# Layer-norm rows of an MLP's token blocks turned by VectorE and DMAs instead of TensorE, in an fp32 adaLN block on one core

## The chip, the cores and the metric

The kernel runs on one core of a Trainium2 chip. The metric is the device time of one execution in microseconds (us). Three runs of the kernel before gave a median of 1103.63 us (1103.35 to 1103.67).

## What is computed

One transformer block with adaptive layer norms, on 2048 tokens of width 448, in fp32. The part that matters here is its second half:

```python
h = _layernorm(x, axis=-1) * (1 + cb) + sb          # x: 2048 x 448
y = _layernorm(h, axis=-1)                          # a second norm, inside the MLP
g = _gelu(jnp.einsum("bsd,df->bsf", y, w1) + b1)    # F = 1792
x = x + gb * (jnp.einsum("bsf,fd->bsd", g, w2) + b2)
```

The first half is a softmax attention with 16 heads of 28 columns over all 2048 tokens. Its code and its order are not touched by the change.

## The kernel before, in words

**Tiling.** The 2048 tokens are four blocks of 512 (`b` = 0 to 3), and a block is four tiles of 128 tokens (`t`). The residual rows of a block stay in SBUF in `acc[b]`, tokens on partitions. Every fp32 product is made of two fp32r parts, a rounded `hi` and a rest `lo`, as three products: hi·hi, hi·lo and lo·hi.

**The MLP phase** runs from about 792 us to the end. The list `seq` has 56 steps, 14 per block: step `n` is block `b`, slice `i` of the hidden width. In a step TensorE first does `mlp1(b, i)`, 11 matrix products (L396) of the turned rows `yT[b]` with a slice of w1, and then `mlp2`, 12 products (L1438 to L1440), for the slice of two steps earlier (`LAG = 2`). Between them, off TensorE: ScalarE applies the GELU to the PSUM tile of `mlp1` (L1394), then `hi` is copied (L1397, on ScalarE in block 0, on VectorE in blocks 1 to 3) and VectorE subtracts to get `lo` (L1398). At a block's last slice, which falls in step 1 of the next block, VectorE adds the four PSUM tiles of `mlp2` to `acc[b]` (L1444) into buffers `xn`, and SyncE stores them (L1445). The PSUM pair tiles `s1` and `s0` are then free for `mlp2` of the next block, which starts in step 2.

**The rows of the next block** are prepared by `ln2_stages(b + 1)`, whose `stage(i)` is called in step `i` of block `b`. In the table `plan`: `stat(0, t)` takes the statistics of `acc` (L200, L201), with the reciprocal root on GpSimd (L207) after the fourth; `mid(t)` normalises (L217) and GpSimd multiplies by `1 + cb` and adds `sb` (L1123, L1124); `stat(1, t)` and `fin(t)` do the second norm, and `fin` copies the last 64 columns once more to columns 448 to 511 (L1129); `addb(t)` lets GpSimd add the row `b2·gb` to `acc` (L1132). An instruction goes to its engine's queue in the order of the program and starts when its own waits are over.

**Turning the rows.** `mlp1` needs features on partitions. `chunk(k)`, for `k` = 0 to 3, takes 128 columns: four TensorE transposes with an identity into one PSUM tile (L277), then ScalarE's copy to `hi` (L1155) and VectorE's subtract to `lo` (L1157, L1159; for `k` = 3, where only 64 columns are real, `hi` fills the lower 64 partitions and `lo` the upper 64). In a block's step 13, chunks 0 and 1 stand on TensorE between `mlp1` and `mlp2`, and chunks 2 and 3 after `mlp2`, ahead of the next block's first `mlp1`.

**Weights.** In block 0 the last slices of w1 and w2 are still being prepared, one or two items a step, by `w_prep.step()`: SyncE loads rows into one of three buffers `raw` (L1175 to L1178 for w1, L1196 for w2). For w1 ScalarE copies `hi` (L1187) and VectorE subtracts (L1188). For w2 VectorE multiplies by `gb` (L1206), ScalarE copies `hi` (L1208) and VectorE subtracts (L1209). The last two of the 30 items are rows of w2, in steps 12 and 13.

**Buffers.** Four buffers `xn` go round for the normalised rows and for the output rows. The buffer `slot_e1` holds half of the attention's output weights until the last `project` in step 8 of block 0.

Of the kernel before, what the change touches and what calls it, by code (L numbers as in the profile page):

```python
# [13 lines left out]
F32 = mybir.dt.float32  # L14
F32R = mybir.dt.float32r
AF = mybir.ActivationFunctionType
ALU = mybir.AluOpType
# [5 lines left out]
D = 448  # L23
# [3 lines left out]
NC = 4  # L27
NB = S // 512
# [16 lines left out]
def tile_adaln_block(ctx: ExitStack, tc: tile.TileContext, x, wqkv, wo, w1, b1, w2, b2, c, w_mod, out):  # L45
    nc = tc.nc
    pe, act, dve, pool, sp = nc.tensor, nc.scalar, nc.vector, nc.gpsimd, nc.sync
# [13 lines left out]
    def ps_tile(key, n=1):  # L61
        return ps_pools[key][1].tile([128, 512], F32, tag=key, name=nm(key), bufs=n)
# [7 lines left out]
    dr = ctx.enter_context(tc.tile_pool(name="dr", bufs=1, space=DRAM))  # L70
# [47 lines left out]
    def f(t):  # L118
        return t.bitcast(F32)
# [78 lines left out]
    def ln_stat(mv, t, src):  # L198
        st = sbt("st", [128, 6], bufs=2)
        dve.bn_stats(out=st, in_=src)  # L200
        dve.bn_aggr(out=mv[:, t, :], in_=st)  # L201

    def ln_rstd(mv, n):
        ve = sbt("ve", [128, 4], bufs=2)
        dve.tensor_scalar(out=ve[:, :n], in0=mv[:, :n, 1], scalar1=EPS, scalar2=None, op0=ALU.add)
        rs = sbt("rs", [128, 4], bufs=2)
        pool.tensor_tensor(out=rs[:, :n], in0=ve[:, :n], in1=neg_half[:, :n], op=ALU.pow)  # L207
        return [(mv[:, t, 0:1], rs[:, t : t + 1], rs) for t in range(n)]
# [7 lines left out]
    def normalise(dst, src, mr):  # L216
        dve.tensor_scalar(out=dst[:, :D], in0=src, scalar1=mr[0], scalar2=mr[1], op0=ALU.subtract, op1=ALU.mult)  # L217

    def xn_t():
        return sbt("xn", [128, 512], bufs=4)  # L220
# [54 lines left out]
    def transposes(p, xs, k):  # L275
        for t in range(4):
            pe.transpose(p[:, t * 128 : (t + 1) * 128], xs[t][:, k * 128 : (k + 1) * 128], ident)  # L277
# [40 lines left out]
    for k in range(NC):  # L318
        for j in range(2):
            rs_, cs = mod_part(k, j, 2)  # L320
# [413 lines left out]


    rows = {}
    drow = dr.tile([4, D], F32, tag="drow", name="drow", bufs=1)

    mod = {}
# [65 lines left out]
    for n, i in (  # L805
# [7 lines left out]
        p, ts = firsts[n]  # L813
# [3 lines left out]
    for b in range(NB):  # L817
# [12 lines left out]
        for n, (tb, kind, g) in enumerate(tasks):  # L830
# [9 lines left out]
            k = n - (6, 4, 4, 4)[b]  # L840
# [5 lines left out]
            if kind < 2:  # L846
                fn = qk_task(tb, kind, g, firsts[n] if b == 0 and n < 3 else None)
# [254 lines left out]
    yT = {}  # L1102

    def ln2_stages(b):
        h2 = []
        ys = []

        mv = {}
        mr = {}

        def stat(which, t):
            if t == 0:
                mv[which] = sbt("mv", [128, 4, 2], bufs=2)
            ln_stat(mv[which], t, acc[b][:, t, :] if which == 0 else h2[t])
            if t == 3:
                mr[which] = ln_rstd(mv[which], 4)

        def mid(t):
            yt = xn_t()
            ys.append(yt)  # L1120
            y = yt[:, :D]
            normalise(y, acc[b][:, t, :], mr[0][t])
            pool.tensor_tensor(out=y, in0=y, in1=rows["cb"], op=ALU.mult)  # L1123
            pool.tensor_tensor(out=y, in0=y, in1=rows["sb"], op=ALU.add)  # L1124
            h2.append(y)

        def fin(t):
            normalise(ys[t], h2[t], mr[1][t])
            dve.tensor_copy(ys[t][:, D:512], ys[t][:, 384:D])  # L1129

        def addb(t):
            pool.tensor_tensor(out=acc[b][:, t, :], in0=acc[b][:, t, :], in1=rows["b2g"], op=ALU.add)  # L1132

        plan = {}
        for t in range(4):
            plan.setdefault(t, []).append(lambda t=t: stat(0, t))
            plan.setdefault(4 + t, []).append(lambda t=t: mid(t))
            plan.setdefault(6 + t, []).append(lambda t=t: stat(1, t))
            plan.setdefault(10 + t // 2, []).append(lambda t=t: fin(t))
            plan.setdefault(10 + t, []).append(lambda t=t: addb(t))  # L1140

        def stage(i):
            for fn in plan.get(i, ()):
                fn()

        def chunk(k):
            if b not in yT:
                tiles = [
                    sb.tile([128, 512], F32R, tag=YTAGS[(7 * b + n) % len(YTAGS)], name=nm("y"), bufs=1) for n in range(7)
                ]  # L1150
                yT[b] = (lambda k: tiles[k] if k < 3 else tiles[6], lambda k: tiles[3 + k])
            p = ps_o() if b and k == 3 else ps_mx()
            transposes(p, ys, k)
            hi = yT[b][0](k)
            act.copy(hi, p)  # L1155
            if k < 3:
                dve.tensor_tensor(out=yT[b][1](k), in0=p, in1=f(hi), op=ALU.subtract)  # L1157
            else:
                dve.tensor_tensor(out=hi[64:128], in0=p[64:128], in1=f(hi)[64:128], op=ALU.subtract)  # L1159

        return stage, chunk

# [285 lines left out]
    for n in range(len(seq) + LAG):  # L1448
        if n < len(seq):
            b, i = seq[n]  # L1450
            if n:
                mlp1(b, i)
            for fn in tail.pop(n, ()):
                fn()
            for _ in range(2 if n % 2 else 1):
                w_prep.step()
            if b + 1 < NB:
                lnst[b + 1][0](i)
        ahead = n < len(seq) and i == NFT - 1 and b + 1 < NB
# [45 lines left out]
```

## Time and profile before

| What | us |
|---|---|
| median of three runs | 1103.63 |
| the profiled execution, its time | 1103.82 |
| its span, first to last instruction | 1101.7 |
| MLP phase, from the first `mlp1` (792.1) to the end | 309.6 |
| PE busy in the whole span | 1094.3 |
| DVE / ACT / POOL busy in the whole span | 798.9 / 697.3 / 196.8 |

TensorE's granted clock is 1.00 in all slices. In a timeline a row is: start, duration, engine, line, operation, output from inputs, shapes, how many were merged, and in brackets the idle time before it with what ended it. Successive matmuls overlap in the records: a row's duration is longer than the step to the next row's start, so the path is read from starts. In a row of groups the last fields are the count, then the busy sum and the mean of one in ns, then the idle time before the group.

### The profile page before, as it was taken

The numbers are of one execution on the slowest core, as the hardware profiler recorded it, in microseconds if no ns is written. First come the engines' busy times: TensorE is split into PE (matmuls) and PEld (weight loads), VectorE is DVE, ScalarE is ACT, GpSimd is POOL, SyncE is SP. The second block draws the span as 40 slices with busy tenths as digits, with TensorE's granted clock in tenths as the row PEclk, the third lists the DMA queues.
The fourth block names the chain that finished last, engine by engine and source line by source line (L and its number), as shares of the span: only waits on it lengthen the run. The fifth ranks groups of instructions, "written<-read, shape, count | busy, mean of one in ns | idle before, by whom it ended". The sixth has DMA issues, their size and how long they took to land.

```text
span 1101.7 us, 20731 instructions
## 1 busy us (share of the span) xinstructions
PE 1094.3 (99%) x8303; PEld 665.3 (60%) x8303; DVE 798.9 (73%) x1382; ACT 697.3 (63%) x883; POOL 196.8 (18%) x201
## 2 busy tenths in 40 slices
PE   9999999999999999999999999999999999999998
PEld 6756675444444444444444444554488888888887
DVE  6968788999999989988888888574655644444322
ACT  4655667888888888888888888678933411211210
POOL 1543332210000000000000000116123214023000
PEclk9999999999999999999999999999999999999999
DMA  9553354221222201231211313111451000000000
GB/s 311 199 191 106 99 183 138 60 64 33 75 76 61 76 28 40 69 102 47 69 48 38 98 42 99 57 31 59 146 144 50 27 34 1 15 20 1 34 1 34
DMA packets 51094, 82.67 MB, mean 75 GB/s; under 512 B 13327, under 2 KB 19878, under 8 KB 50986
## 3 DMA queue, kind: packets, MB, share of 16 engines
q1 hardware_dynamic: 50514, 80.61, 23.9%
q8 instruction: 65, 1.06, 0.4%
q10 hardware_dynamic: 148, 0.46, 0.1%
q0 software_dynamic: 336, 0.28, 0.1%
q14 instruction: 31, 0.25, 0.1%
HBM read 56.25 MB, written 26.75 MB: 75 GB/s over the span
## 4 chain that ended last, share of the span: by engine, by line
PE 97%; DVE 1%; ACT 0%; DMA 0%; issue 0%; ACTq 0%; DVEq 0%
PE s L1348 23%; PE o L1303 23%; PE m L396 17%; PE pa L396 9%; PE m L476 8%; PE s L1439 3%; PE s L1440 3%; PE s L1438 3%; PE s L476 2%; PE t L1439 1%; PE t L1440 1%; PE t L1438 1%; PE o L277 1%; DVE mxp L481 0%; PE ma L476 0%; PE m L277 0%
## 5 line engine op out<-in xcount | busy, mean ns | idle before, releaser
L481 DVE TENSOR_REDUCE mxp<-m 128x1 f32<-128x512 f32 x555 | 359.9, 686 | 64.7 <-PE m L476 46.9
L1348 PE MATMUL s<-slot_b,slot_a 28*128 28x512 f32 (+1 forms) x3072 | 356.7, 423 | 0.0
L1348 PEld LDWEIGHTS s<-slot_b,slot_a 28*128 28x128 f32 (+1 forms) x3072 | 211.2, 183 | 175.8 <-ACT slot_c L1361 96.4
L476 PE MATMUL m<-kh,qh 28*128 28x512 f32 x607 | 227.0, 468 | 0.4 <-DVE mxp L481 0.3
L1361 ACT ACTIVATE slot_c<-s 128x1024 f32<-128x1024 f32 x170 | 174.8, 1028 | 51.5 <-PE s L1348 50.8
L1303 PE MATMUL o<-slot_c,v 128*32 128x512 f32 x680 | 178.9, 605 | 0.0
L1394 ACT ACTIVATE full<-m,b_col 128x512 f32<-128x512 f32 x56 | 38.6, 689 | 205.3 <-PE m L396 188.5
L686 DVE TENSOR_REDUCE mxp<-s 128x2 f32<-128x1024 f32 x107 | 131.2, 1226 | 5.0
L1303 PE MATMUL o<-slot_c1h,v 128*32 128x512 f32 x512 | 134.7, 605 | 0.0
L1303 PE MATMUL o<-slot_c0h,v 128*32 128x512 f32 x508 | 133.6, 605 | 0.0
L1361 ACT ACTIVATE slot_c1h<-s 128x1024 f32<-128x1024 f32 x128 | 130.7, 1021 | 0.0
L1361 ACT ACTIVATE slot_c0h<-s 128x1024 f32<-128x1024 f32 x127 | 130.5, 1027 | 0.0
L1397 DVE CAST hi<-full 128x512 fp32r<-128x512 f32 x42 | 18.6, 443 | 121.1 <-ACT full L1394 121.1
L1361 ACT ACTIVATE slot_d<-s 128x1024 f32<-128x1024 f32 x86 | 88.4, 1028 | 25.2 <-PE s L1348 24.9
L476 PEld LDWEIGHTS m<-kh,qh 28*128 28x128 f32 x607 | 90.8, 182 | 15.2 <-DVE mxp L481 13.3
L1303 PE MATMUL o<-slot_d,v 128*32 128x512 f32 x344 | 90.5, 605 | 0.4 <-ACT osb L1267 0.4
L1061 POOL TENSOR_TENSOR osb<-osb,osb 128x512 f32<-128x512 f32 x16 | 20.6, 1284 | 363.5 <-DMA osb<-drec 247.1
L1398 DVE TENSOR_TENSOR lo<-full,hi 128x512 fp32r<-128x512 f32 x56 | 43.0, 768 | 26.6 <-ACT hi L1397 22.6
L396 PE MATMUL m<-y,slot_a 128*128 128x512 f32 x160 | 60.7, 395 | 0.0
L481 DVE TENSOR_REDUCE mxp<-ma 128x1 f32<-128x512 f32 x61 | 39.5, 682 | 13.2 <-PE m L476 8.0
L1303 PEld LDWEIGHTS o<-slot_c,v 128*32 128x32 f32 x680 | 24.5, 108 | 39.0 <-issue 36.4
L650 DVE CUSTOM_DVE_ANT_0 slot_d0i<-m,slot_d0i 128x512 f32<-128x512 f32 x54 | 37.3, 691 | 14.3 <-PE m L476 11.6
(351 smaller groups left out, 1835.7 us busy)
## 6 DMA issues: line engine op xcount, KB each, us to landing
slot_b<-d SPq DMA_DIRECT2D x32, 256.0 KB
slot_a<-d SPq DMA_DIRECT2D x32, 256.0 KB
d<-lo SPq DMA_DIRECT2D x28, 256.0 KB
d<-hi SPq DMA_DIRECT2D x16, 256.0 KB
osb<-drec SPq DMA_DIRECT2D x15, 256.0 KB
out_dram<-xn SPq DMA_DIRECT2D x16, 224.0 KB
raw<-in_B_w_dram SPq DMA_DIRECT2D x14, 224.0 KB
qh<-d SPq DMA_DIRECT2D x12, 256.0 KB
```

Of the source, the lines that this page charges most:

```text
L396: pe.matmul(p, a, b, start=(i == 0), stop=(i == len(terms) - 1))
L476: pe.matmul(m, qh_sb[(g, qt)][js, i * 128 : (i + 1) * 128], k[js, :], start=True, stop=True)
L481: dve.tensor_reduce(out=mxp[(g, qt)][:, i, j, cch : cch + 1], in_=m, op=ALU.max, axis=AX.X)
L686: dve.tensor_reduce(out=mxp[(g, qt)][:, i, j : j + 2, cch], in_=t, op=ALU.max, axis=AX.X)
L1303: pe.matmul(o[32 * j : 32 * j + 32, :], v_sb[kt // 4][:, kt % 4, 4 * g + j, :], p[j // 2][:, j % 2, :], start=(kt == 0), stop=(kt == NKT - 1),
L1348: pe.matmul(s2[:, jj, :], ks[rows_, kp, kc], qs[rows_, qp, :], start=(term == 0), stop=(term == 2))
L1361: act.activation(pt[hf], s2, AF.Exp, scale=SCALE)
L1394: act.activation(gf, p, AF.Gelu_apprx_tanh, bias=b1_col[:, i : i + 1])
L1398: dve.tensor_tensor(out=glo, in0=gf, in1=f(ghi), op=ALU.subtract)
L1438: pe.matmul(pp, ghi[:, ts], w_hi, start=(m == 0), stop=False)
L1439: pe.matmul(pp, ghi[:, ts], w_lo, start=False, stop=False)
L1440: pe.matmul(pp, glo[:, ts], w_hi, start=False, stop=(m == NFT - 1))
```

## The change

In blocks 1 to 3 `chunk` no longer uses TensorE. Three steps take the place of the 16 transposes of a block:

- `turn(t)`: VectorE transposes the 32x32 squares of a token tile, 128 x 448, into `slot_e1` (tile `turned[0]`), ordered so that the four token tiles of a column group lie side by side.
- `send()`: four DMAs, one for each quarter of the partitions, write it to a DRAM scratch `y_dr` of 448 x 512. Each moves 32 x 14 runs of 128 numbers, 512 bytes.
- `fetch()`: five DMAs read `y_dr` back by rows into four buffers `xn`, features on partitions.

`chunk(k)` then copies and subtracts from these SBUF tiles, with runs of 32 numbers put in their places (shape 4x4x32).

The norm is placed anew. For block 1 (prepared in block 0) the last two `stat(1, t)` move to stage 8, all `fin` to stage 9, all `turn` and `send` to stage 10, `fetch` to stage 11. For blocks 2 and 3 everything is two tiles a stage: statistics in 0 and 1, `mid` in 2 and 3, `stat(1)` in 4 and 5, `fin` in 6 and 7, `turn` in 7 and 8, `send` in 8, `fetch` in 9. The second copy of 64 columns in `fin` goes for blocks 1 to 3. The bias rows of blocks 1 and 2 are added in steps 10 to 13 of the own block; block 3's stay in block 2.

```diff
+    y_dr = dr.tile([D, 512], F32, tag="y_dr", name="y_dr", bufs=1)
...
         def fin(t):
             normalise(ys[t], h2[t], mr[1][t])
-            dve.tensor_copy(ys[t][:, D:512], ys[t][:, 384:D])
+            if not b:
+                dve.tensor_copy(ys[t][:, D:512], ys[t][:, 384:D])
+
+        def turn(t):
+            if t == 0:
+                turned.append(slot("e1", [128, 14, 4, 32], F32))
+            dve.transpose(turned[0][:, :, t, :], ys[t][:, :D].rearrange("p (c j) -> p c j", j=32))
+
+        def send():
+            for r in range(4):
+                sp.dma_start(
+                    y_dr.rearrange("(c i) (r n) -> r i c n", i=32, r=4)[r],
+                    turned[0][32 * r : 32 * r + 32].rearrange("i c t j -> i c (t j)"),
+                )
+
+        def fetch():
+            for k in range(NC):
+                turned.append(xn_t())
+                for h in range(1 if k < 3 else 2):
+                    rs_ = slice(0, 128) if k < 3 else slice(64 * h, 64 * h + 64)
+                    sp.dma_start(turned[-1][rs_], y_dr[128 * k : min(128 * k + 128, D), :])
...
-            plan.setdefault(t, []).append(lambda t=t: stat(0, t))
-            plan.setdefault(4 + t, []).append(lambda t=t: mid(t))
-            plan.setdefault(6 + t, []).append(lambda t=t: stat(1, t))
-            plan.setdefault(10 + t // 2, []).append(lambda t=t: fin(t))
-            plan.setdefault(10 + t, []).append(lambda t=t: addb(t))
+            own = 20 if 0 < b < NB - 1 else 0
+            at_stage = (
+                (t, 4 + t, 6 + t, 10 + t // 2, 10 + t),
+                (t, 4 + t, min(6 + t, 8), 9, 30 + t),
+                (t // 2, 2 + t // 2, 4 + t // 2, 6 + t // 2, own + 10 + t),
+            )[min(b, 2)]
...
+            if b:
+                plan.setdefault(10 if b < 2 else 7 + t // 2, []).append(lambda t=t: turn(t))
+        if b:
+            plan.setdefault(10 if b < 2 else 8, []).append(send)
+            plan.setdefault(11 if b < 2 else 9, []).append(fetch)
...
-            p = ps_o() if b and k == 3 else ps_mx()
-            transposes(p, ys, k)
             hi = yT[b][0](k)
+            lo = yT[b][1](k) if k < 3 else hi
+            rs_ = slice(0 if k < 3 else 64, 128)
+            if b:
+                p = turned[1 + k].rearrange("p (r t j) -> p r t j", r=4, t=4)
+                hi, lo = (x.rearrange("p (t r j) -> p r t j", r=4, t=4) for x in (hi, lo))
+            else:
+                p = ps_mx()
+                transposes(p, ys, k)
             act.copy(hi, p)
...
+            dve.tensor_tensor(out=lo[rs_], in0=p[rs_], in1=f(hi)[rs_], op=ALU.subtract)
...
             if b + 1 < NB:
                 lnst[b + 1][0](i)
+            if b:
+                lnst[b][0](20 + i)
```

**TensorE, end of block 1.** Before, these rows stand behind the 12 products of `mlp2` in step 13 of block 1; `m` and `o` are PSUM tiles, `ident` the identity, `xn` the four token tiles of block 2, and the last two rows are the first `mlp1` of block 2.

```order
L1440 MATMUL s_2734_11806<-slot_d0i_11368,lo_12119 128x448
L277 MATMUL m_2802_12222<-ident_77,xn_11874 128x128
L277 MATMUL m_2802_12222<-ident_77,xn_11908 128x128
L277 MATMUL m_2802_12222<-ident_77,xn_11946 128x128
L277 MATMUL m_2802_12222<-ident_77,xn_11983 128x128
L277 MATMUL o_12229<-ident_77,xn_11874 128x128
L277 MATMUL o_12229<-ident_77,xn_11908 128x128
L277 MATMUL o_12229<-ident_77,xn_11946 128x128
L277 MATMUL o_12229<-ident_77,xn_11983 128x128
L396 MATMUL m_2804_12236<-y_12189,slot_b_2501_10656 128x512
L396 MATMUL m_2804_12236<-y_12189,slot_a_2502_10657 128x512
```

In the changed kernel the same place reads as follows (its lines L1472 to L1474 are L1438 to L1440 of before).

```order
L1473 MATMUL s_2740_11812<-slot_b1h_11371,hi_12127 128x448
L1474 MATMUL s_2740_11812<-slot_d0i_11369,lo_12128 128x448
L396 MATMUL m_2806_12221<-y_12194,slot_b_2501_10657 128x512
L396 MATMUL m_2806_12221<-y_12194,slot_a_2502_10658 128x512
L396 MATMUL m_2806_12221<-y_12195,slot_b_2501_10657 128x512
```

The eight transposes are gone, and so are the eight that stood ahead of this `mlp2`; `mlp1` of the next block follows `mlp2` directly.

**SyncE, end of block 0.** Before: the last loads of weights (`raw`) and the first store of output rows.

```order
L1175 DMA raw_11495<-in_B_w_dram 128x256
L1177 DMA raw_11536<-in_B_w_dram 64x256
L1178 DMA raw_11536<-in_B_w_dram 64x256
L1196 DMA raw_11576<-in_B_w_dram 128x448
L1196 DMA raw_11580<-in_B_w_dram 128x448
L1445 DMA out_dram<-xn_11772 128x448
```

In the changed kernel (L1212 is L1178 of before, L1230 is L1196, L1479 is L1445):

```order
L1212 DMA raw_11541<-in_B_w_dram 64x256
L1142 DMA y_dr<-slot_e_2685_11544 32x14x128 x4
L1230 DMA raw_11585<-in_B_w_dram 128x448
L1230 DMA raw_11589<-in_B_w_dram 128x448
L1152 DMA xn_11591<-y_dr 128x512
L1152 DMA xn_11593<-y_dr 128x512
L1152 DMA xn_11595<-y_dr 128x512
L1152 DMA xn_11597<-y_dr 64x512 x2
L1479 DMA out_dram<-xn_11773 128x448
```

The four writes of `send` now stand ahead of the last two loads of w2, and the five reads of `fetch` behind them.

**VectorE, steps 9 and 10 of block 0.** Before: the statistics' end (`ve`), the GELU's `lo` of step 10, a weight item (`slot_c1h`), and the first two `fin` of block 1 (L217, L1129).

```order
L200 BN_STATS st_11497<-xn_11386 128x6
L201 BN_AGGR mv_11315<-st_11497 128x2
L205 TENSOR_SCALAR ve_11500<-mv_11315 128x4
L1398 TENSOR_TENSOR lo_11531<-full_11528,hi_11530 128x512
L1188 TENSOR_TENSOR slot_c1h_11492<-raw_11489,slot_c_2674_11491 128x256
L217 TENSOR_SCALAR xn_11217<-xn_11217,mv_11315,rs_11502 128x448
L1129 COPY xn_11217<-xn_11217 128x64
L217 TENSOR_SCALAR xn_11264<-xn_11264,mv_11315,rs_11502 128x448
L1129 COPY xn_11264<-xn_11264 128x64
```

In the changed kernel (L1432 is L1398 of before, L1222 is L1188):

```order
L217 TENSOR_SCALAR xn_11218<-xn_11218,mv_11316,rs_11461 128x448
L217 TENSOR_SCALAR xn_11265<-xn_11265,mv_11316,rs_11461 128x448
L217 TENSOR_SCALAR xn_11320<-xn_11320,mv_11316,rs_11461 128x448
L217 TENSOR_SCALAR xn_11387<-xn_11387,mv_11316,rs_11461 128x448
L1432 TENSOR_TENSOR lo_11536<-full_11533,hi_11535 128x512
L1222 TENSOR_TENSOR slot_c1h_11500<-raw_11497,slot_c_2677_11499 128x256
L1138 STREAM_TRANSPOSE slot_e_2685_11544<-xn_11218 128x14x32
L1138 STREAM_TRANSPOSE slot_e_2685_11544<-xn_11265 128x14x32
L1138 STREAM_TRANSPOSE slot_e_2685_11544<-xn_11320 128x14x32
L1138 STREAM_TRANSPOSE slot_e_2685_11544<-xn_11387 128x14x32
```

The four `fin` have moved ahead of step 10's `lo`, with the statistics a step earlier still, and the four turns stand where the first two `fin` stood.

More of the change, by code (lines that the diff above doesn't have):

```diff
@@ L1125, in mid @@
             h2.append(y)
+        turned = []
         def fin(t):
             normalise(ys[t], h2[t], mr[1][t])
-            dve.tensor_copy(ys[t][:, D:512], ys[t][:, 384:D])
+            if not b:
[16 more added lines that the diff above has]
+                    sp.dma_start(turned[-1][rs_], y_dr[128 * k : min(128 * k + 128, D), :])
         def addb(t):
@@ L1135, in ln2_stages @@
         for t in range(4):
-            plan.setdefault(t, []).append(lambda t=t: stat(0, t))
-            plan.setdefault(4 + t, []).append(lambda t=t: mid(t))
-            plan.setdefault(6 + t, []).append(lambda t=t: stat(1, t))
-            plan.setdefault(10 + t // 2, []).append(lambda t=t: fin(t))
-            plan.setdefault(10 + t, []).append(lambda t=t: addb(t))
+            own = 20 if 0 < b < NB - 1 else 0
[4 more added lines that the diff above has]
+            )[min(b, 2)]
+            for i, fn in zip(at_stage, (lambda t=t: stat(0, t), lambda t=t: mid(t), lambda t=t: stat(1, t), lambda t=t: fin(t), lambda t=t: addb(t))):
+                plan.setdefault(i, []).append(fn)
+            if b:
[3 more added lines that the diff above has]
+            plan.setdefault(11 if b < 2 else 9, []).append(fetch)
         def stage(i):
@@ L1151, in chunk @@
                 yT[b] = (lambda k: tiles[k] if k < 3 else tiles[6], lambda k: tiles[3 + k])
-            p = ps_o() if b and k == 3 else ps_mx()
-            transposes(p, ys, k)
             hi = yT[b][0](k)
+            lo = yT[b][1](k) if k < 3 else hi
[6 more added lines that the diff above has]
+                transposes(p, ys, k)
             act.copy(hi, p)
[L1156 to L1159, printed above, removed]
+            dve.tensor_tensor(out=lo[rs_], in0=p[rs_], in1=f(hi)[rs_], op=ALU.subtract)
         return stage, chunk
```

## Prediction, on record before the changed kernel was run

> **What bounds the kernel now.** I read the page's busy shares first, then its chain of work that ended last.
>
> ```profile
> PE 1094.3 (99%) x8303; PEld 665.3 (60%) x8303; DVE 798.9 (73%) x1382; ACT 697.3 (63%) x883; POOL 196.8 (18%) x201
> PE 97%; DVE 1%; ACT 0%; DMA 0%; issue 0%; ACTq 0%; DVEq 0%
> ```
>
> TensorE is busy 99% of the span and is 97% of the chain. So what leaves TensorE's queue shortens the run, unless what comes next isn't ready. The change touches only the MLP phase, so next I read TensorE's timeline where block 1 hands over to block 2.
>
> ```profile
> 946.73 1.03 PE L277 MATMUL m<-ident,xn 128*128 128x128 f32 x8
> 947.52 0.45 PE L1438 MATMUL s<-slot_d0i,hi 128*128 128x448 f32 x1
> ...
> 950.05 0.60 PE L277 MATMUL m<-ident,xn 128*128 128x128 f32 x4
> 950.49 0.60 PE L277 MATMUL o<-ident,xn 128*128 128x128 f32 x4
> 950.84 0.48 PE L396 MATMUL m<-y,slot_b 128*128 128x512 f32 x1
> ```
>
> By starts, eight transposes take 947.52 - 946.73 = 0.79 us and the other eight 950.84 - 950.05 = 0.79 us: **1.58 us for a block**, with no idle time. At the first boundary there is some.
>
> ```profile
> 878.99 0.50 PE L396 MATMUL m<-y,slot_b 128*128 128x512 f32 x1 [0.36 <-DVE y L1157]
> ...
> 881.64 0.37 PE L1438 MATMUL s<-slot_e,hi 128*128 128x448 f32 x1
> ```
>
> There `mlp1(1, 0)` already waits 0.36 us for the rows, so ScalarE and VectorE, not only TensorE, set that boundary.
>
> **What goes, and what is late next.** At boundary 1 to 2 (2 to 3 is the same code) `mlp1` would start at 950.84 - 1.58 = 949.26. What it needs then is made by ScalarE
>
> ```profile
> 946.98 0.69 ACT L1394 ACTIVATE full<-m,b_col 128x512 f32<-128x512 f32 x1 [4.32 <-PE m L396]
> 947.57 1.07 ACT L1155 CAST y<-m 128x512 fp32r<-128x512 f32 x2
> 950.69 0.59 ACT L1155 CAST y<-m 128x512 fp32r<-128x512 f32 x1 [2.05 <-PE m L277]
> ```
>
> and by VectorE:
>
> ```profile
> 948.24 0.69 DVE L1398 TENSOR_TENSOR lo<-full,hi 128x512 fp32r<-128x512 f32 x1
> 948.85 1.28 DVE L1157 TENSOR_TENSOR y<-m,y 128x512 fp32r<-128x512 f32 x2
> ```
>
> With tiles that are there, ScalarE copies from 947.57, about 0.54 apart: 948.1, 948.6, 949.2, 949.7. VectorE subtracts from 948.85, 0.61 apart, so the fourth starts at 950.68 and ends at 951.37. TensorE asks for it tenth: at (881.64 - 878.99) / 11 = 0.24 us a product, nine of them take it to 951.4. The two meet; I keep 0.08 for the hand-over and count a **gain of 1.5 us at each of these two boundaries**.
>
> At boundary 0 to 1 the copies don't start earlier, because a weight item stands in front of them:
>
> ```profile
> 877.11 0.57 ACT L1208 CAST slot_e<-full 128x448 fp32r<-128x448 f32 x1 [1.29 <-DVE full L1206]
> 877.58 1.55 ACT L1155 CAST y<-m 128x512 fp32r<-128x512 f32 x3
> ```
>
> and on VectorE:
>
> ```profile
> 878.25 1.88 DVE L1157 TENSOR_TENSOR y<-m,y 128x512 fp32r<-128x512 f32 x3
> 880.16 0.69 DVE L1159 TENSOR_TENSOR y<-o,y 64x512 fp32r<-64x512 f32 x1
> ```
>
> The first copy ends at about 878.15, the last subtract still at 880.85. The last two of the eleven products need that subtract: 880.9 + 2 x 0.24 = 881.4 in place of 881.64. **Gain 0.3 us**, not 1.9: the transposes and the 0.36 turn into a wait for ScalarE and VectorE.
>
> **The new operations.** Nearest rows:
>
> ```profile
> L205 DVE TENSOR_SCALAR ve<-mv 128x4 f32<-128x4 f32 x11 | 1.8, 168 | 0.3
> L525 DVE STREAM_TRANSPOSE full<-m 128x32 f32<-128x32 f32 x16 | 3.2, 203 | 0.1
> L217 DVE TENSOR_SCALAR xn<-acc,mv,rs 128x448 f32<-128x448 f32 x18 | 10.0, 557 | 1.5 <-POOL rs L207 1.5
> L458 ACT COPY v<-pa 128x448 f32<-128x448 f32 x15 | 8.0, 534 | 3.6 <-PE pa L396 3.6
> L1035 ACT COPY full<-m 128x448 f32<-128x448 f32 x8 | 4.3, 533 | 14.4 <-PE m L396 14.4
> ```
>
> A turn of 448 numbers isn't in the trace. From 4 to 32 numbers costs 35 ns, 1.25 ns each, which gives 0.168 + 444 x 0.00125 = 0.72 us. Bounds: 0.56 (L217, the same shape), and 14 x 0.203 = 2.8 if each square pays alone. I take 0.72, whose row is the same operation. L458 writes runs of 28 to places 32 apart and takes 534 ns, a plain copy of as many numbers (L1035) 533: runs of 32 in `chunk` should cost ScalarE nothing. For VectorE I take that over; its bound is rival 2. That the sources now lie in SBUF changes little: L1398 with two SBUF sources takes 0.69, as L1157 does.
>
> The Trainium skill, "VectorE: DVE Perf Modes", sections "The three transpose paths" and "Rules for kernel authors", speaks against the change: it advises TensorE for a 128x128 transpose into PSUM and gives VectorE 311 ns for 128x128. An estimate from that page is 3.5 x 0.311 = 1.09 us for a turn; four turns would end 1.5 us later than by my row, and the sum would not change, since the cover below is longer.
>
> For the DMAs, rows of two short stretches (890.5 to 894, four stores of output rows; 717 to 718.3, 8 KB in pieces of 64 bytes) and of SyncE's waits:
>
> ```profile
> q1 hardware_dynamic: 576, 0.92, 72.0%
> ...
> q1 hardware_dynamic: 139, 0.02, 10.6%
> ...
> SPq L1056 <- DMA drec<-den: 27.0, 15, 3.1
> ```
>
> In the first, 0.72 x 16 x 3.5 = 40 us over 576 packets are 70 ns for some 1600 bytes; in the second 0.106 x 16 x 1.3 = 2.2 us over 139 are 16 ns for some 160. 512 bytes lie between, by proportion at 29 ns. `send` has 4 x 32 x 14 = 1792 packets: 1792 x 29 ns / 16 = **3.3 us** (bounds 1.8 and 7.8). SyncE waits 27.0 / 15 = 1.8 us for a DMA of 8 KB that it has issued (L1056); with the issue I count 2.1, so `send` is done 5.4 us after the last turn.
>
> **Is it hidden in block 0?** This is the tight place, and these are its rows of before:
>
> ```profile
> 860.82 1.51 DVE L1398 TENSOR_TENSOR lo<-full,hi 128x512 fp32r<-128x512 f32 x1 [1.26 <-ACT hi L1397]
> 862.25 1.37 DVE L1188 TENSOR_TENSOR slot_c1h<-raw,slot_c 128x256 fp32r<-128x256 f32 x1
> ...
> 871.45 0.62 DVE L1206 TENSOR_TENSOR full<-raw,row_gb 128x448 f32<-128x448 f32 x1
> ```
>
> with ScalarE and GpSimd:
>
> ```profile
> 874.47 0.69 ACT L1394 ACTIVATE full<-m,b_col 128x512 f32<-128x512 f32 x1 [1.80 <-PE m L396]
> 860.63 5.27 POOL L1132 TENSOR_TENSOR acc<-acc,row_b2g 128x448 f32<-128x448 f32 x4
> ```
>
> GpSimd's bias rows stretched VectorE here (1.51 for a `lo` that takes 0.69 elsewhere). They leave block 0, so `lo` ends at 861.5, L1188 at 861.9, four turns at 864.8, `send` at 870.2. Behind `send` in SyncE's queue wait the last two loads of w2; the first lands after `send`'s data, about 870.8 with its own 0.6 us, and L1206 wants it at 871.45. After L1206 there is 1.8 us more until ScalarE needs to be free for the GELU at 874.47 (871.45 + 0.62 + 0.57 = 872.64). `fetch` starts at 870.2 and its first tile is there 2.7 us later, 872.9, wanted at 877.58; the last, with 1 MB at the stores' 0.92 MB in 2.5 us, at 875.2, wanted at 879.1. So it is hidden, with **2.5 us to spare**; at the upper bound of the packets (4.5 us more) the boundary comes 2 us later.
>
> In blocks 1 and 2 `send` stands in stage 8, four stages ahead of the copies, and a stage takes (891.62 - 881.64) / 2 = 5.0 us. Nothing but stores 20 us later waits behind it. GpSimd has all eight bias rows of blocks 2 and 3 in block 2, 8 x 1.32 = 10.5 us in which a `lo` takes 1.5, but `lo` is used two steps, 10 us, later: nothing.
>
> The statistics of step 1, now two tiles, stand ahead of the additions that free `s1`:
>
> ```profile
> 889.41 0.18 DVE L201 BATCH_NORM_AGGREGATE mv<-st 128x2 f32<-128x6 f32 x1
> 889.62 2.22 DVE L1444 TENSOR_TENSOR xn<-s,acc 128x448 f32<-128x448 f32 x4
> ```
>
> and TensorE's first use of the tile:
>
> ```profile
> 891.62 0.37 PE L1438 MATMUL s<-slot_v,hi 128*128 128x448 f32 x1
> ```
>
> They start some 0.85 us later, 890.47; the second ends at 891.65 where TensorE comes at 891.62. I charge 0.1 us in blocks 1 and 2 (bounds 0 and 0.4). `mid`, two stages earlier, writes the buffers `xn` that these rows are stored from, so VectorE can wait there for their stores: the second row is made at 891.65, its store done by my 2.1 + 0.6 us at 894.4, and step 2's `lo` ends at about 893.7. Behind that 0.7 us on VectorE stands only the next GELU's copy, a step later. Nothing.
>
> **Sum.** 0.3 + 1.5 + 1.5 - 0.2 = 3.1 us off the profiled execution's 1103.82 (span 1101.7 and 2.1 around it), 1100.7; the median is 0.19 lower, so **1100.5 us**.
>
> **Rivals.** *1. Block 0's chain is late.* Turns and `send` take 8.3 us by my rows. Beyond 2.5 us more, each further us delays L1206, L1208, the GELU and the boundary. At the packets' bound 2 us are lost: 1102.5. From 5.6 us more (turns of 2.1 us each, say) the gain is gone, and at 14 x 0.203 per turn, 8.3 us more, it costs 5.8: 1106.3, slower. For it: neither operation has a row at this size. Against: both bounds lie far from the nearest rows. The same page of the Trainium skill has a trap in "The three transpose paths": a plain DMA that transposes by strides is 19 times slower where the innermost destination stride is large. By that an estimate for `send` is 19 x 2.5 = 47 us and some 90 us lost over three blocks; here 512 bytes run on without a stride, no row shows it, and I give it 0.01. *2. Runs of 32 are slow on VectorE.* If the four subtracts took 1.2 us each, not 0.61 apart, the last would end 2.4 us later, at all boundaries: 3 x 2.4 - 3.1, 1107.7, slower; it decides at 0.87 us apart. Against: L458. *3. TensorE's gap only changes its name.* The saved 1.58 us become a wait at every boundary as at the first, since the last subtract stands just where TensorE asks for it: 1103.6. Against: ScalarE's copies start at 947.57 by the GELU and no longer stop for TensorE between the second and the third.
>
> **How the numbers follow.** A measurement here can tell about 0.2%, 2.2 us. Forecast 0.72 (1099.5 to 1101.4; the lower end has the whole 1.58 twice and 0.9 at the first). Rival 1 0.14 (the trap's 0.01 in it): half of it up to 1103, half slower. Rival 2 0.06, slower. Rival 3 0.08. Faster 0.74 with a part of rival 1, same 0.13, slower 0.13. From 1099.5 to 1103.0 lie the forecast and the milder half of rival 1, 0.79.
>
> **What would show it.** In the changed profile: no L277 after block 0; the turns near 0.72 us; `mlp1(2, 0)` directly behind `mlp2`, with TensorE idle under 0.2 us there, and idle 1.5 to 2 us, for ScalarE and VectorE, at boundary 0 to 1; L1206 of step 12 not waiting for its `raw`. A wait of ScalarE for a DMA at a boundary, or subtracts over 0.8 us, would prove me wrong.

## The result and the profile after

| | before | after |
|---|---|---|
| median, us | 1103.35 (1102.65 to 1103.67, 7 runs) | 1099.95 (1099.43 to 1101.74, 7 runs) |
| ratio, 95% interval | | 0.9974 (0.9965 to 0.9984) |
| the profiled execution, its time | 1103.82 | 1099.75 |

The change takes 3.4 us off by the medians and 2.9 by the ratio (1.8 to 3.9 by its interval); 3.1 were forecast. The ratios and medians here and below leave disturbed runs out, and a ratio is the record's own, not the quotient of two medians (here 0.9969). The page of the changed kernel opens with the same picture as before: TensorE is busy 99% of the span, 6.2 us less in all, and carries 96% of the chain.

```profile
PE 1088.1 (99%) x8255; PEld 658.3 (60%) x8255; DVE 805.1 (73%) x1382; ACT 697.6 (64%) x883; POOL 198.7 (18%) x201
PE 96%; DVE 2%; DMA 1%; ACT 1%; issue 0%; SPq 0%; DVEq 0%; ACTq 0%
```

The shares say little. The result is read at the boundaries: from the end of `mlp1(b, 13)` to the first product of the `mlp2` in the next block's step 0, that is `mlp2` of 12 products, `mlp1(b + 1, 0)` of 11, and before the change 16 transposes. By starts on TensorE's timeline, in us:

| | block 0 | 0 to 1 | block 1 | 1 to 2 | block 2 | 2 to 3 | block 3 | sum |
|---|---|---|---|---|---|---|---|---|
| before | 82.20 | 7.37 | 65.09 | 6.75 | 65.09 | 6.75 | 72.16 | 305.41 |
| after | 81.82 | 7.20 | 65.18 | 5.35 | 65.27 | 5.35 | 72.25 | 302.42 |

(Block 0 counts from the first `mlp1`, block 3 to the start of the last product.) So 2.99 of the profile's 4.07 us lie here: 1.40 at each of the two later boundaries, 0.17 at the first and 0.38 in block 0, less 0.36 that blocks 1 to 3 take longer. Another 0.92 us is the first `mlp1`, which starts at 791.15 in place of 792.07 after code that the change doesn't touch; the experiments' kernels start it between 791.5 and 793.1, so one profile differs from another by as much.

**Boundary 1 to 2.** TensorE after the change:

```profile
947.59 0.37 PE L1474 MATMUL s<-slot_d0i,lo 128*128 128x448 f32 x1
947.80 0.39 PE L396 MATMUL m<-y,slot_b 128*128 128x512 f32 x1
...
949.19 0.85 PE L396 MATMUL m<-y,slot_b 128*128 128x512 f32 x3
950.13 0.50 PE L396 MATMUL m<-y,slot_a 128*128 128x512 f32 x1
950.47 0.40 PE L396 MATMUL m<-y,slot_b 128*128 128x512 f32 x1
950.70 0.37 PE L1472 MATMUL s<-slot_e,hi 128*128 128x448 f32 x1
```

`mlp1(2, 0)` follows `mlp2` directly, 0.21 us after it. Nine products run at 0.23 us; the tenth starts 0.94 us after the group of three ahead of it, where three steps of 0.23 would be 0.69, and the eleventh 0.34 behind the tenth. The tenth needs the last subtract on VectorE:

```profile
946.32 0.43 DVE L1431 CAST hi<-full 128x512 fp32r<-128x512 f32 x1 [3.78 <-ACT full L1428]
946.86 0.69 DVE L1432 TENSOR_TENSOR lo<-full,hi 128x512 fp32r<-128x512 f32 x1
947.47 2.61 DVE L1193 TENSOR_TENSOR y<-xn,y 128x512 fp32r<-128x512 f32 x4
```

Four subtracts take 2.61 us, 0.65 apart, and end at 950.08. Ahead of them on VectorE's queue stand the two steps on GELU's 14th tile (`hi`, `lo`).

**Boundary 0 to 1.** TensorE:

```profile
875.21 0.37 PE L1474 MATMUL s<-slot_d0i,lo 128*128 128x448 f32 x1
876.94 0.50 PE L396 MATMUL m<-y,slot_b 128*128 128x512 f32 x1 [1.36 <-ACT y L1192]
...
879.60 0.50 PE L396 MATMUL m<-y,slot_a 128*128 128x512 f32 x1 [0.19 <-DVE y L1193]
```

The transposes' time has become 1.36 us of waiting for ScalarE's first copy, and 0.19 for the last subtract. ScalarE, which copies 0.545 us apart:

```profile
873.17 0.69 ACT L1428 ACTIVATE full<-m,b_col 128x512 f32<-128x512 f32 x1 [1.75 <-PE m L396]
873.89 0.62 ACT L1431 CAST hi<-full 128x512 fp32r<-128x512 f32 x1
875.80 0.56 ACT L1242 CAST slot_e<-full 128x448 fp32r<-128x448 f32 x1 [1.29 <-DVE full L1240]
876.27 2.18 ACT L1192 CAST y<-xn 128x512 fp32r<-128x512 f32 x4
```

Its copies stand behind the last weight item's conversion (L1242), and that behind VectorE's product (L1240). VectorE's rows show both the turns and what L1240 stands behind:

```profile
860.46 2.22 DVE L1138 STREAM_TRANSPOSE slot_e<-xn 128x448 f32<-128x448 f32 x4
...
869.53 0.69 DVE L1432 TENSOR_TENSOR lo<-full,hi 128x512 fp32r<-128x512 f32 x1 [3.64 <-ACT hi L1431]
870.19 0.62 DVE L1240 TENSOR_TENSOR full<-raw,row_gb 128x448 f32<-128x448 f32 x1
...
874.54 0.69 DVE L1432 TENSOR_TENSOR lo<-full,hi 128x512 fp32r<-128x512 f32 x1 [2.47 <-ACT hi L1431]
875.15 0.62 DVE L1240 TENSOR_TENSOR full<-raw,row_gb 128x448 f32<-128x448 f32 x1
```

The second L1240 comes right behind the GELU's `lo`, which VectorE waits 2.47 us for. The chain is GELU, `hi` on ScalarE, `lo`, product, conversion, copies, each in the queue's order.

**The new DMAs.** SyncE's issues, then the DMA engines by stretches, then the packets of 864 to 866:

```profile
862.71 3.04 SPq L1142 DMA_DIRECT2D y_dr<-slot_e  x4
865.85 2.20 SPq L1230 DMA_DIRECT2D raw<-in_B_w_dram  x2
869.08 2.42 SPq L1152 DMA_DIRECT2D xn<-y_dr  x5
```

```profile
864.00:866.00 2.00, 2.00 (x11) 1.80 (x10) 1.36 (x3) 1.11 (x3) 0.00 (x0) 1.00 0.97 172
866.00:868.00 2.00, 2.00 (x11) 1.60 (x10) 0.00 (x0) 0.00 (x0) 0.00 (x0) 1.00 0.99 221
```

```profile
q1 hardware_dynamic: 689, 0.34, 96.6%
```

The last three columns of a stretch are the granted clock, the DMA engines' share and GB/s. While only `send` runs, all 16 engines are busy at 172 GB/s: 0.966 x 16 x 2.00 us over 689 packets are 45 ns for a packet of 512 bytes.

### The profile page after: what moved, and what is told of

It reads as the page before. It is cut to its first block, busy times and chain, and to the rows that moved or that the text cites. A ratio compares the mean times of both kernels' runs of the same rounds, so it can differ in the third digit from the quotient of the medians.

```text
span 1097.5 us, 20709 instructions
## 1 busy us (share of the span) xinstructions
PE 1088.1 (99%) x8255; PEld 658.3 (60%) x8255; DVE 805.1 (73%) x1382; ACT 697.6 (64%) x883; POOL 198.7 (18%) x201
## 4 chain that ended last, share of the span: by engine, by line
PE 96%; DVE 2%; DMA 1%; ACT 1%; issue 0%; SPq 0%; DVEq 0%; ACTq 0%
PE s L1382 23%; PE o L1337 23%; PE m L396 16%; PE pa L396 9%; PE m L476 8%; PE s L1472 3%; PE s L1473 3%; PE s L1474 3%; PE s L476 2%; PE t L1473 1%; PE t L1474 1%; PE t L1472 1%; DVE y L1193 1%; DMA slot_c<-in_w_mod_dram 1%; PE o L277 1%; DVE mxp L481 0%
## 5 line engine op out<-in xcount | busy, mean ns | idle before, releaser
L1432 DVE TENSOR_TENSOR lo<-full,hi 128x512 fp32r<-128x512 f32 x56 | 46.0, 822 | 29.7 <-ACT hi L1431 25.1
```

The costliest lines, as they stand in the source:

```text
L1432: dve.tensor_tensor(out=glo, in0=gf, in1=f(ghi), op=ALU.subtract)
```

## Experiments

Each time stands beside runs of the kernel before on the same chip (medians 1103.40 for e1, e2, e3 and e5, 1103.27 for e4, e6, e7 and e8, 1103.24 for e9 and e10); the ratio is to these. The boundaries of each, in us:

| kernel | block 0 | 0 to 1 | block 1 | 1 to 2 | block 2 | 2 to 3 | sum with block 3 |
|---|---|---|---|---|---|---|---|
| e1, block 1 alone | 81.79 | 7.21 | 65.18 | 6.75 | 65.09 | 6.75 | 304.93 |
| e2, blocks 2, 3 alone | 82.18 | 7.37 | 65.37 | 5.34 | 65.20 | 5.34 | 302.93 |
| e3, placement alone | 81.81 | 7.37 | 65.39 | 6.75 | 65.33 | 6.75 | 305.56 |
| e4, turn a stage later | 81.79 | 9.92 | 66.48 | 5.35 | 65.20 | 5.33 | 306.21 |
| e5, weight item earlier | 81.80 | 5.47 | 65.14 | 5.35 | 65.24 | 5.35 | 300.59 |
| e6, subtracts first | 81.99 | 5.16 | 65.20 | 4.99 | 65.23 | 4.99 | 299.72 |
| e7, send twice | 81.79 | 11.05 | 65.50 | 5.34 | 65.19 | 5.34 | 306.34 |
| e8, all three orders | 81.80 | 5.00 | 65.08 | 5.00 | 65.08 | 5.00 | 299.12 |
| e9, e8 with block 1 on TensorE | 81.79 | 6.75 | 65.08 | 5.00 | 65.08 | 5.00 | 300.85 |
| e10, before with new orders | 81.81 | 6.75 | 65.09 | 6.75 | 65.09 | 6.75 | 304.39 |

### The change in parts: e1, e2, e3

In e1 and e2 only some blocks take the new path and placement; in e3 all have the new placement and bias rows, and all transposes stay on TensorE.

```diff
+TURN = (1,)        # e1;  (2, 3) in e2;  () in e3
...
-            if b:
+            if b in TURN:
                 p = turned[1 + k].rearrange("p (r t j) -> p r t j", r=4, t=4)
```

e1 expected: 

> Only block 1 is turned by VectorE and DMAs; blocks 2 and 3 go back to TensorE's transposes and to the old placement. Theory A (the gain is TensorE's transposes at the boundaries 1 to 2 and 2 to 3, 1.4 us each; at 0 to 1 ScalarE's and VectorE's weight work takes their place): boundary 0 to 1 as in the changed kernel, about 0.2 us shorter than before; the other two boundaries 6.75 us as before; in all 0.2 to 0.6 us under the kernel before, not to be told from it. Theory B (a third of the gain comes from block 0, by the norm pulled together and the bias rows that leave it): 1 us or more under the kernel before, with block 0 shorter than 81.8 us.

Measured 1103.16 us (1102.53 to 1104.22), ratio 0.9999 (0.9990 to 1.0009).

e2 expected: 

> Only blocks 2 and 3 are turned by VectorE and DMAs; block 1 goes back to TensorE and to the old placement in block 0. Theory A: both later boundaries 5.35 us as in the changed kernel, boundary 0 to 1 7.37 us as before; 2.5 to 3.0 us under the kernel before, nearly all of the change's gain. Theory B: only two thirds of the gain, 2 us or less.

Measured 1100.75 us (1100.14 to 1101.46), ratio 0.9976 (0.9967 to 0.9986).

e3 expected: 

> The new placement of norm and bias rows for blocks 1 to 3, but every block's rows turned by TensorE as before (with the second copy of 64 columns in fin); no turn, send or fetch. Theory A: no gain; 0 to 0.3 us over the kernel before, from VectorE's two statistics ahead of the additions that free the PSUM tiles in step 1 of blocks 1 and 2 (the step's mlp2 2.50 us, not 2.40). Theory B: 1 us or more under the kernel before.

Measured 1104.10 us (1103.14 to 1105.08), ratio 1.0006 (0.9997 to 1.0015).

What follows: the gain is that of blocks 2 and 3, whose boundaries shrink by 1.41 us each in e2's profile. Block 1's turn removes 16 transposes and brings 0.16 us at its boundary. The placement brings nothing, and costs 0.30 and 0.24 us in blocks 1 and 2 by e3's profile; e3's time is 0.7 us over the kernel before by the medians, where theory A had at most 0.3, and its interval still holds 1.

### What sets the first boundary: e5

The changed kernel, with the last weight item one step earlier, in step 12 with the one before it:

```diff
-            for _ in range(2 if n % 2 else 1):
+            for _ in range(2 if n % 2 or n == 12 else 1):
                 w_prep.step()
```

Expected: 

> The changed kernel with the last weight item of w2 prepared in step 12, not 13, so that it no longer stands ahead of the copies of block 1's rows on ScalarE and VectorE. Theory A (at boundary 0 to 1 the copies wait for that item): TensorE's idle 1.36 us at that boundary goes to under 0.4 us, the boundary from 7.20 to about 5.6 us, 1.4 to 1.9 us under the changed kernel. Rival (the fetched rows land only just before the copies): ScalarE waits for a DMA there and less than 0.5 us is gained.

Measured 1098.95 us (1098.15 to 1099.65), ratio 0.9959 (0.9946 to 0.9972). The boundary falls from 7.20 to 5.47 us, and TensorE's 1.36 us of waiting for ScalarE are gone; 0.20 for the last subtract stay:

```profile
878.92 0.50 PE L396 MATMUL m<-y,slot_a 128*128 128x512 f32 x1 [0.20 <-DVE y L1193]
```

So the weight item, not the turned rows, held ScalarE's copies in the changed kernel. The boundary gives 1.73 us, inside theory A's 1.4 to 1.9; the medians (1098.95 against 1099.95) give 1.0, below it.

### How much cover the new chain has: e4 and e7

e4: block 1's turns, `send` and `fetch` one stage later, behind the last two loads of w2.

```diff
-                plan.setdefault(10 if b < 2 else 7 + t // 2, []).append(lambda t=t: turn(t))
+                plan.setdefault(11 if b < 2 else 7 + t // 2, []).append(lambda t=t: turn(t))
...
-            plan.setdefault(10 if b < 2 else 8, []).append(send)
-            plan.setdefault(11 if b < 2 else 9, []).append(fetch)
+            plan.setdefault(11 if b < 2 else 8, []).append(send)
+            plan.setdefault(12 if b < 2 else 9, []).append(fetch)
```

Expected: 

> Block 1's four turns and the send come one MLP step later (stage 11), the fetch in stage 12; blocks 2 and 3 as in the change. Theory A (block 0's chain has little to spare, as the trace of the changed kernel reads: turned rows sent from 863.6 to 868.8, first fetched tile wanted by ScalarE at 876.27): the send is done near 874.5, the first fetched tile lands near 877.2 and the last near 880, so ScalarE's copies at the boundary 0 to 1 wait for the fetched tiles instead of the w2 conversion, and the kernel takes 1.6 us more than the changed one: 1101.5 us (1100.9 to 1102.2). Rival B (several us to spare): 1099.9 us, with the copies where they were.

Measured 1103.77 us (1102.35 to 1105.46), ratio 1.0003 (0.9995 to 1.0012): the whole gain is lost. Theory A has the place right, and not the size (1101.5 us). The profiled execution, at 1105.46 us, is the slowest of the eleven. ScalarE now waits for the fetched tiles, twice:

```profile
878.84 1.28 ACT L1192 CAST y<-xn 128x512 fp32r<-128x512 f32 x2 [0.56 <-DMA xn<-y_dr]
880.98 1.30 ACT L1192 CAST y<-xn 128x512 fp32r<-128x512 f32 x2 [0.86 <-DMA xn<-y_dr]
```

and TensorE for ScalarE:

```profile
879.51 0.50 PE L396 MATMUL m<-y,slot_b 128*128 128x512 f32 x1 [2.02 <-ACT y L1192]
...
881.65 0.80 PE L396 MATMUL m<-y,slot_b 128*128 128x512 f32 x1 [0.70 <-ACT y L1192]
882.24 0.63 PE L396 MATMUL m<-y,slot_a 128*128 128x512 f32 x1
882.67 1.48 PE L396 MATMUL m<-y,slot_b 128*128 128x512 f32 x3
883.95 0.63 PE L396 MATMUL m<-y,slot_a 128*128 128x512 f32 x1
```

TensorE's idle time is 2.02 + 0.70 us in place of 1.55, 1.2 us more. But the boundary grows by 2.72 us and block 1 by 1.30, 4.0 in all. Nearly all of the rest is in the products' step: 0.43 us here ((883.95 - 882.67) / 3), where it is 0.23 elsewhere. TensorE's stretches, with the granted clock third from the end, show why:

```profile
877.50:880.00 2.50, 0.49 (x2) 1.00 0.95 338
880.00:881.00 1.00, 0.95 (x4) 0.85 0.45 135
881.00:887.00 6.00, 5.35 (x13) 0.50 0.00 0
887.00:888.00 1.00, 1.00 (x5) 0.73 0.00 0
```

The clock was granted at half for some 6.8 us after the idle time, from about 880.7 to 887.5. The second wait began only at 881.65 - 0.70 = 880.95, after the drop, so the one of 2.02 us was enough. Neither theory had that.

e7: the turned rows are sent twice in each block, the second time to a scratch that nobody reads.

```diff
-            for r in range(4):
-                sp.dma_start(
-                    y_dr.rearrange("(c i) (r n) -> r i c n", i=32, r=4)[r],
...
+            for d in (y_dr, y_dr2):
+                for r in range(4):
+                    sp.dma_start(
+                        d.rearrange("(c i) (r n) -> r i c n", i=32, r=4)[r],
```

Expected: 

> The turned rows are sent twice in blocks 1 to 3, the second time to another scratch in DRAM that nobody reads. Theory A (a send occupies the DMA engines for some 5.2 us, and the w2 load queued behind it in block 0 is wanted soon after): in block 0 the w2 piece lands near 875 instead of 870, VectorE's product, ScalarE's conversion, GELU of product 13 and the copies follow each other late, and the boundary 0 to 1 grows by 2.2 to 4.2 us (3.2): 1103.1 us (1102.1 to 1104.2); blocks 1 and 2 have nothing behind the send that is wanted soon and stay at 5.35 us a boundary. Rival B (queues run beside each other, or there are several us of cover): within 0.5 us of the changed kernel, 1099.9 us.

Measured 1105.01 us (1102.41 to 1105.79), ratio 1.0011 (1.0002 to 1.0019). Rival B falls: the second `send` costs, and of the boundaries at the first alone (11.05 us, while 1 to 2 and 2 to 3 stay at 5.34). The boundary grows by 3.85 us, inside theory A's 2.2 to 4.2, but the time lies above its 1104.2, and the reasons are two. VectorE shows the first:

```profile
874.56 0.63 DVE L1242 TENSOR_TENSOR full<-raw,row_gb 128x448 f32<-128x448 f32 x1 [4.04 <-DMA raw<-in_B_w_dram]
```

The product of the w2 rows (L1240 of the changed kernel) comes at 874.56 in place of 870.19, held by the load behind the doubled `send`. ScalarE's copies follow at

```profile
878.78 2.17 ACT L1194 CAST y<-xn 128x512 fp32r<-128x512 f32 x4
```

in place of 876.27. The MLP starts 0.32 us later in this execution, so the w2 rows are 4.05 us late and the copies 2.19: 1.9 us of cover took the rest. TensorE waits 3.59 us:

```profile
879.45 0.80 PE L396 MATMUL m<-y,slot_b 128*128 128x512 f32 x1 [3.59 <-ACT y L1194]
```

The second reason is the clock again, at half from 878 to 884.8:

```profile
875.50:878.00 2.50, 0.36 (x2) 1.00 0.80 254
878.00:884.00 6.00, 4.55 (x11) 0.50 0.02 5
884.00:885.00 1.00, 1.00 (x5) 0.58 0.00 0
885.00:886.00 1.00, 1.00 (x7) 1.00 0.00 0
```

The runs tell the two reasons apart. One of the eleven kept a mean granted clock of 1.00 and took 1102.41 us, 2.5 over the changed kernel's median; the other ten, at 0.996 to 0.998, took 1103.91 to 1105.79. So by this one run the wait alone brings the time into theory A's 1102.1 to 1104.2, and the half clock adds 1.5 to 3.4 us.

### The last subtract, and all that is left: e6 and e8

e6: the changed kernel, with the two steps on GELU's 14th tile written behind the four subtracts.

```diff
+        def split():
+            (dve.tensor_copy if b else act.copy)(ghi, gf)
+            dve.tensor_tensor(out=glo, in0=gf, in1=f(ghi), op=ALU.subtract)
...
+        if i < NFT - 1 or b == NB - 1:
+            split()
+        else:
+            held.append(split)
...
             for k in range(2, NC):
                 lnst[b + 1][1](k)
+            held.pop()()
```

Expected: 

> The changed kernel, with VectorE's (and in block 0 ScalarE's) two steps on GELU's 14th tile written behind the four subtracts at the end of blocks 0 to 2. Theory A (the fourth subtract, 0.24 us late for TensorE, stands behind these two steps on VectorE): the four subtracts start 0.7 us earlier at the boundaries 1 to 2 and 2 to 3, and the boundary takes 5.11 instead of 5.35 us; at 0 to 1 ScalarE's copy is gone from ahead of the copies but the w2 conversion sets their start, so up to 0.2 us there: 0.5 to 0.7 us less in all, 1099.3 us. Rival B (the subtracts are held by ScalarE's copies, 0.545 us apart): 0 to 0.1 us less, 1099.9 us.

Measured 1097.53 us (1097.33 to 1097.85), ratio 0.9946 (0.9933 to 0.9958): 2.4 us below the changed kernel where theory A had 0.5 to 0.7. The boundaries 1 to 2 and 2 to 3 fall by 0.36 each (5.35 to 4.99), more than the 0.24 of theory A: 23 products at their own pace take just this. The surplus is at the first boundary, 7.20 to 5.16, and VectorE's rows there show its cause:

```profile
872.44 0.62 DVE L1240 TENSOR_TENSOR full<-raw,row_gb 128x448 f32<-128x448 f32 x1
874.85 0.63 DVE L1243 TENSOR_TENSOR slot_e<-full,slot_e 128x448 fp32r<-128x448 f32 x1 [1.79 <-ACT slot_e L1242]
875.39 2.61 DVE L1193 TENSOR_TENSOR y<-xn,y 128x512 fp32r<-128x512 f32 x4
```

With `lo` gone from ahead of it, the last weight item's product runs at 872.44 instead of 875.15. The w2 rows had landed in time; what held L1240 was its place on VectorE behind an instruction that waited for ScalarE. So e5 and e6 take away the same wait in two ways.

e8: e5's and e6's edits together, and in step 1 of blocks 1 and 2 the two statistics behind `mlp2`'s additions that free `s1`.

```diff
-            if b + 1 < NB:
+            if b + 1 < NB and not (b and i == 1):
                 lnst[b + 1][0](i)
...
             mlp2(*seq[n - LAG])
+        if n < len(seq) and i == 1 and 0 < b < NB - 1:
+            lnst[b + 1][0](i)
```

Expected: 

> The changed kernel, with the last weight item one step earlier, the two steps on GELU's 14th tile behind the subtracts, and in blocks 1 and 2 the second pair of statistics behind mlp2's additions that free s1. If the three costs are separate (1.7 us at the boundary 0 to 1, 0.24 at each of three boundaries for the fourth subtract, 0.1 in each of blocks 1 and 2 for the additions), the MLP takes 299.7 us in the trace instead of 302.42, and the kernel 1097.4 to 1098.2 us, below both kernels. If the third cost is not the statistics' place, 0.2 us of it is missing and mlp2(1,0) and mlp2(2,0) still last 2.50 us.

Measured 1097.31 us (1097.16 to 1097.87), ratio 0.9945 (0.9932 to 0.9959), below both kernels and just under the 1097.4 to 1098.2 that were expected; from e6 it can't be told apart by its time. In the profile all three boundaries take 5.00 us, blocks 1 and 2 65.08, and TensorE has no idle row in the MLP. `mlp2(1, 0)` and `mlp2(2, 0)` last 2.41 us each; they last 2.40 before, 2.50 and 2.51 after the change. VectorE's additions start right behind the GELU's `lo` in e8, 0.61 us after its start (885.84 - 885.23):

```profile
885.23 0.69 DVE L1434 TENSOR_TENSOR lo<-full,hi 128x512 fp32r<-128x512 f32 x1
885.84 2.21 DVE L1485 TENSOR_TENSOR xn<-s,acc 128x448 f32<-128x448 f32 x4
```

In the changed kernel they start behind the statistics, 2.29 us after the start of that `lo`, 1.68 later than in e8:

```profile
886.65 0.69 DVE L1432 TENSOR_TENSOR lo<-full,hi 128x512 fp32r<-128x512 f32 x1
...
888.94 2.21 DVE L1478 TENSOR_TENSOR xn<-s,acc 128x448 f32<-128x448 f32 x4
```

### Does the turn pay, or the order: e9 and e10

e9 is e8 with block 1 turned by TensorE (`TURN = (2, 3)`, as in e2, but with the change's placement kept). e10 is the kernel before with e5's and e6's edits and nothing of the change.

e9 expected: 

> The version with all three reorderings, but block 1's rows turned by TensorE as before the change (blocks 2 and 3 by VectorE and DMAs). Theory A (the first boundary gained little only because the weight item and the split of GELU's 14th tile stood ahead of the copies; with these gone the 16 transposes are worth their 1.58 us there too): boundary 0 to 1 takes 6.6 us instead of 5.00, and the kernel 1.6 us more than with all three: 1098.9 us (1098.4 to 1099.5). Rival B (block 1's turn is worth nothing wherever it stands): 1097.3 us.

Measured 1098.84 us (1098.09 to 1099.22), ratio 0.9960 (0.9948 to 0.9973).

e10 expected: 

> The kernel before the change, with TensorE's transposes everywhere, and only the last weight item one step earlier and the split of GELU's 14th tile behind the subtracts. Theory A (the reorderings take away waits that stand only beside the transposes, and TensorE still works 1.58 us at each boundary): 0 to 1 goes from 7.37 to 6.6 to 6.75 us, 1 to 2 and 2 to 3 from 6.75 to no less than 6.58: 0.7 to 1.1 us less in all, 1102.3 us (1101.7 to 1102.8). Rival B (the reorderings alone are worth what they brought on top of the change, 2.4 us): 1100.9 us.

Measured 1102.82 us (1102.04 to 1103.42), ratio 0.9995 (0.9986 to 1.0004).

Theory A holds in both, with 6.75 us at the first boundary where it had 6.6 and 6.6 to 6.75; e10's time is at the upper end of its 1101.7 to 1102.8. With the order mended, block 1's turn is worth 1.5 us of time and 1.75 at its boundary (6.75 in e9, 5.00 in e8). The order alone, with the transposes left on TensorE, takes 0.62 us off the first boundary, nothing off the others, and 0.4 us off the time, which its interval can't tell from nothing. By medians, then: the order alone 0.4, the change alone 3.4, both 6.0 us (1103.27 to 1097.31 in e8).

The transposes cost more than I read from their starts: 1.75 instead of 1.58 us. The switch from them to products is in it; in e9 the step after the first product is 878.16 - 877.84 = 0.32 us, not 0.23:

```profile
877.48 0.60 PE L278 MATMUL o<-ident,xn 128*128 128x128 f32 x4
877.84 0.48 PE L397 MATMUL m<-y,slot_b 128*128 128x512 f32 x1
878.16 0.40 PE L397 MATMUL m<-y,slot_a 128*128 128x512 f32 x1
```

## Why the prediction was right, point by point

**Boundaries 1 to 2 and 2 to 3: forecast 1.5 each, measured 1.40.** The mechanism is the one forecast: `mlp1` directly behind `mlp2`, with the last subtract late by a little. Two sizes were off and nearly cancel: the transposes' 1.75 us in place of 1.58, and a hand-over of 0.35 (5.35 against e8's 5.00) in place of 0.08. The 0.35 are a tenth product 0.25 us late (0.94 - 0.69) and 0.11 more for the step behind it (0.34 in place of 0.23). Four subtracts 0.65 us apart, where I took 0.61, explain 0.16 of the lateness.

**Boundary 0 to 1: forecast 0.3, measured 0.17.** The working itself gave 0.24 (881.64 - 881.4). Right in kind: idle 1.55 us (forecast 1.5 to 2), with the weight item ahead of the copies. My reading stopped at that item on ScalarE. e5 and e6 show that one place on VectorE held it, and that 2 us lay there.

**The statistics ahead of the additions: forecast 0.1 in blocks 1 and 2, measured 0.10 and 0.11** on `mlp2(1, 0)` and `mlp2(2, 0)`, and taken back by e8.

**The turn: forecast 0.72 us, measured 0.555** (2.22 / 4). The slope from rows of 4 and 32 numbers was a poor base; the row of the same shape (0.56, my lower bound) was the better one. The Trainium skill, "VectorE: DVE Perf Modes", "The three transpose paths", led to an estimate of 1.09 us, scaled up from a figure that the page gives for bf16; the measurement is half of that.

**`send`: forecast 3.3 us of data, measured 5.0** (1792 packets of 45 ns on 16 engines; I took 29). The same section's trap, a plain DMA that transposes by strides and is 19 times slower than the DMA transpose by crossbar where the innermost destination stride is large, didn't appear in runs of 512 bytes.

**The cover in block 0: forecast 2.5 us, measured 1.9** (e7). The two errors above partly cancel: the turns ended earlier, `send` ran longer. In the changed kernel the first L1240 starts 0.66 us after the `lo` ahead of it (870.19 - 869.53), before the change 0.61 (871.45 - 870.84). So `raw` is hidden as forecast, but only just: its last part lands at 870.10 by the trace, and e7 has 0.10 us from that landing to the start. Of the forecast 2.5 us, 0.65 lay ahead of L1206 (871.45 against 870.8) and 1.8 behind it; the measured 1.9 lie all behind it.

**The bias rows and the placement: forecast at nothing, and nothing gained** (e3). The costs of e3 in blocks 1 and 2 are larger than in the changed kernel, 0.30 against 0.09 and 0.24 against 0.18; this wasn't followed.

**The rivals.** The first, a late chain in block 0, didn't happen, but e4 puts it one stage away, at a gain of zero. I priced it as a delay alone; the halved clock adds to that. The second decides at 0.87 us a subtract; 0.65 was measured. The third holds at the first boundary only, where I had put it.

**The sum.** 0.17 + 1.40 + 1.40 less 0.09, 0.18 and 0.09 in blocks 1, 2 and 3 is 2.61 us, where 3.1 were forecast. The trace's 2.99 is nearer to that only by block 0's 0.38 us, which is no term of the forecast; that part of the agreement is luck. Before the change TensorE waits there, at 800 us, for rows of the attention's output that are read back; the waits of that moment in the kernel before:

```profile
PEld m L396 <- DMA slot_c0h<-w: 0.6, 2, 0.4
```

e2 has this wait too (82.18 us in block 0), the others don't. e10, with the placement of before, shows 81.81, so the change isn't needed to be rid of it; why the load is later in some profiles stays open.

## What to carry to other kernels

Moving work off the engine that sets the end is worth what that engine would do next without waiting, so read the queues of the engines that feed it before the edit, not only their busy shares: here two instructions, written some lines later (e6), brought 2.4 us on top of the change's 3.4, while the same edit with e5's brought next to nothing without the change (e10). A wait ahead of an instruction names what ended it, while the cause can be one place earlier in the same queue. And where the covered engine is left idle for some 2 us, price the clock too.

## What the runs showed of the hardware

- **The clock after an idle stretch.** Idle 1.36 and 0.19 us within some 4 us (the changed kernel): the granted clock stays at 1.00. Idle 3.59 us (e7): half from 2.1 us after the idle time began, for 6.8 us. Idle 2.02 us (e4): half from 3.2 us after it began, when TensorE was at work again, for 6.8 us. No run here tells where between 1.36 and 2.02 us the limit lies. The products' step goes from 0.23 to 0.43 us. By the boundary and block 1 together, e7's 2.04 us of added idle time cost 4.2 us and e4's 1.17 cost 4.0. The Trainium skill, "TensorE: Matmul & The Clock Gate", "What's actually happening", states a free-running window of about 3.4 us, half clock after an idle one and full clock after a busy one. The half rate agrees, and the 6.8 us of both runs are two such windows. Its advice in "Why this matters for your kernels", no gap over some 3 us, isn't enough by e4, whose longest gap is 2.02 us.
- **VectorE's transpose of 32x32 squares** in fp32 takes 0.555 us for 128x448, as long as a plain pass over the same shape in the prediction's rows (0.557).
- **Runs of 32 numbers** cost ScalarE's copy 0.545 us and VectorE's subtract 0.65 us a tile; before the change, out of PSUM and without such runs, they took 0.52 (1.55 / 3) and 0.63 (1.88 / 3).
- **SBUF to DRAM in runs of 512 bytes** keeps all 16 DMA engines busy at 172 GB/s. The four stores of output rows in the prediction take the same way with rows of 1792 bytes: 0.92 MB in 0.72 x 3.5 = 2.5 us of all 16 engines, about 365 GB/s.
